# Polysketch attention into a SwiGLU block: the exact 12-bit parts a batch earlier

## Chip, cores and metric

The kernel runs on one core of one Trainium2 chip. The metric is the device time of one execution in microseconds (us). Before the change it is 293.77 us, the median of 3 runs (292.49 to 293.79); the execution that was profiled took 292.29 us, of which the span from first to last instruction is 290.6 us.

## What is computed

Four batches, four heads, 1088 tokens, head size 32. A sketch of rank 8 gives 64 features per token and head; attention with these is linear, and its result x (4352 tokens of 128) goes through a gated feed-forward block of 1536 hidden columns. All inputs and outputs are fp32.

```python
def phi(x):
    a = np.einsum('rd,bhsd->bhsr', S1, x)
    b = np.einsum('rd,bhsd->bhsr', S2, x)
    return np.einsum('bhsi,bhsj->bhsij', a, b).reshape(*x.shape[:-1], r * r)
kv = np.einsum('bhsf,bhsd->bhfd', k_p, v)
z = np.sum(k_p, axis=2)
num = np.einsum('bhsf,bhfd->bhsd', q_p, kv)
den = np.einsum('bhsf,bhf->bhs', q_p, z)[..., None] + 1e-06
# x = (num / den), heads side by side, 4352 x 128
g = x @ w_gate
silu = g * (1.0 / (1.0 + np.exp(-g)))
val = x @ w_val
return silu * val @ w_out
```

## The kernel before

**Blocks, units, downs.** Each batch of tokens is cut into three blocks of 384, 384 and 320 tokens, so that there are twelve; the 1536 hidden columns are twelve chunks of 128. A *unit* is one chunk of one block: a gate product and a value product on TensorE, SiLU on ScalarE, and their product into a slot of `hbuf`. A *down* (L936) multiplies a finished hidden chunk with its 128 rows of `w_out` and adds into the PSUM bank `acc`; after twelve downs of a block, `store` (L967) transposes the bank on VectorE and sends it out. The list `todo` holds hidden chunks that wait for their down, and a lag says how many may wait.

**Three kinds of unit.** `unit` (L903, matmuls at L911) makes both products in true fp32; SiLU is L917, and VectorE multiplies it with the value straight out of PSUM (L928). `cut_unit` (L868) makes a product from parts that hold 12 bits each[...]: a product of differences `xd` by `wd` (L877), then `x1` by `w1` and `x0` by `wb` (L883, L884), which ScalarE (L889) and VectorE (L892) put together into `sum`. With `both=False` only the value is made so and the gate stays fp32 (L879); with `both=True` both are. In either case GpSimd multiplies SiLU and value into `hbuf` (L901)[...]. The parts of weights come from `cut_weights` (L835), four steps for each of four quarter weights: `w1` on ScalarE, `low` on GpSimd, `wb` on ScalarE, `wd` on GpSimd. Those of a block's tokens come from `cut_tokens` (L850): `x1` on ScalarE, `x0` on a given engine (L859), and, after a yield, `xd` on VectorE (L863).

**Banks and buffers.** [...] At first units take g0, g1, g2 (and `acc`) in turn, and `a` and `b`, two banks each, belong to attention. Once `oldest[0]` is set, `bank` (L110) gives the bank that was handed out longest ago among those not held. A `cut_unit` takes three banks, or four with both products. `sg`, SiLU's output, has three buffers.

**Order.** The schedule is by hand[...]. The first batch's units are mixed with its attention and with the reading of the weights; from its 18th unit of the list at L1137 on, each unit has one down. The 23 downs that are left run three at a time in the loop at L1160. Then comes the loop of units at L1177, y = 0 to 107, over the blocks 3, 4, 5, 6, 7, 8, 9, 11, 10.

Attention of the batches 1 to 3 is the generator `attentions` (L563), of which `parts_of` (L1087) runs a piece at a time between units: `turns` (transposes of keys and queries), `features` (key features, L355), `feature_sums` (L521, sums of key features over token groups, four adds on GpSimd), and `query_step` (L706: query products with the sums at L719, reduces at L726, small operations at L735 to L741, feature products at L355 and transposes at L750). When it yields "pe", it has come to work for TensorE: `group` (L1093) then runs `numerators` (L760, matmuls L770, copies into `xT` at L787), `values` (key-value products L366, and L678, which reads the sums `zs`), sketches of the next batch (L332, L320) and `spread_out` (L683). The token columns of a batch after its first 384 exist only after that group. "first" is the mark after the numerators of the second batch's first 384 tokens; before, the loop of downs stops at it.

The three groups stand ahead of y = 12, 36 and 60. Units y < 38 are plain; y 38 to 47 have the value in parts, y 48 to 106 both, and y 107 is plain. The lag is 2 up to y 37 and 5 after. Value weights are cut from y 2, gate weights from y 14. `oldest[0]` is set at y 36.

```python
PLAIN, VALUE = 3 * NCH + 2, 4 * NCH
...
    if y in (NCH, 3 * NCH, 5 * NCH):
        group()
...
    if y < PLAIN or y == END - 1:
        unit(i, j)
    else:
        cut_unit(i, j, both=y >= VALUE)
    lag = LAG if y < PLAIN else min(5, END - y + 1)
```

Of the kernel before, what the change touches and what calls it, by code (L numbers as in the profile page):

```python
# [7 lines left out]
FP32 = mybir.dt.float32  # L8
# [4 lines left out]
AF = mybir.ActivationFunctionType  # L13
ALU = mybir.AluOpType
# [5 lines left out]
def kernel(  # L20
# [28 lines left out]
    nc = tc.nc  # L49
    P = nc.NUM_PARTITIONS  # L50
# [6 lines left out]
    NC = (NX + 3) // 4  # L57
    F = R * R
    NCH = Dff // P
# [7 lines left out]
    steps = [(sum(plan[:s]), n) for s, n in enumerate(plan)]  # L67
# [13 lines left out]
    fpool = ctx.enter_context(tc.tile_pool(name="ffn", bufs=2))  # L81
# [10 lines left out]
    oldest = [False]  # L92
# [41 lines left out]
    wg = const.tile([P, NCH, P], FP32, name="wg")  # L134
# [151 lines left out]
    def run(*gens):  # L286
        for g in gens:
            for _ in g:
                pass
# [231 lines left out]
    def feature_sums(phk):  # L521

        rows = phk[:].rearrange("p c h i j -> p c (h i j)")
        s = apool.tile([P, 4, H * F], FP32, tag="zs", name="zs")
        add = lambda o, a, b: nc.gpsimd.tensor_tensor(out=o, in0=a, in1=b, op=ALU.add)  # L525
        add(s[:], rows[:, 0:4, :], rows[:, 4:8, :])
        add(s[:, 0:2, :], s[:, 0:2, :], s[:, 2:4, :])
        add(s[:, 0, :], s[:, 0, :], s[:, 1, :])
        add(s[:, 0, :], s[:, 0, :], rows[:, 8, :])
        return s[:, 0, :]  # L530

    def turns(b):

        for c in kpieces:
            turn_k(*c)
            if c[1] == NC and b + 1 < B:
                load_k(b + 1)
            yield
        for x0, x1 in ((0, 4 * kpieces[0][1]), (4 * kpieces[0][1], 4 * NC)):
            nc.vector.transpose(out=qT[:, x0:x1, :], in_=qld[:, x0:x1, :])  # L540
            if x1 == 4 * NC and b + 1 < B:
                load_q(b + 1)
            yield
# [19 lines left out]
    def attentions():  # L563
# [25 lines left out]
        for n, (i, c0, c1) in enumerate(((0, 0, 3), (0, 3, 5), (1, 5, 7), (1, 7, 9))):  # L589
# [11 lines left out]
                release("a")  # L601
            if n % 3 != 1:
                yield
        zs = feature_sums(phk)
        for i, _ in enumerate(turns(2)):
            if i % 2:
                yield
# [18 lines left out]
        phk = hbuf[:, NH - 6 :, :].rearrange("p s (n h i j) -> p (s n) h i j", h=1, i=R, j=R)  # L626
        phk = phk.rearrange("p (c h) o i j -> p c (h o) i j", h=H)
        yield from features(phk, fac2, ())
        zs = feature_sums(phk)
        yield from turns(3)  # L630
        yield "pe"
        numerators(1, spread, 3, NC)
        hold("a", "b")
# [2 lines left out]
        kp, qp = wide("a"), wide("b")  # L636
        fac3, copies = sketches([(c0, c1, kp[:, i], qp[:, i]) for i, (c0, c1) in enumerate(kpieces)])
        spread = spread_out(2, kv)
        run_copies(copies, 2)
        yield  # L640
        run_copies(copies, 2)
        release("a", "b")
        yield
        yield from features(phk, fac3, ())
        zs = feature_sums(phk)
        yield from query_step(2, fac2, spread)(0, NC)
        yield "pe"
        numerators(2, spread, 0, NC)
        kv = bank()
# [145 lines left out]

    LAG = 2
    hidden = {}
    acc = {}  # L800
    todo = []
# [14 lines left out]
    def whole(ap):  # L816
        return ap.bitcast(FP32)
# [14 lines left out]
                for k in range(2):  # L832
                    yield [x[:, k] for x in t]

    def cut_weights(w, at, steps):  # L835

        def put(at, f, **args):
            steps.setdefault(at, []).append(lambda: f(**args))  # L838

        for c, (w1, wb, wd) in enumerate(homes(w)):  # L840
            src = w[:, 3 * c : 3 * c + 3, :]
            low = fpool.tile([P, 3, P], FP32, tag="sgl", name="low", bufs=6)[:]
            w_parts[id(w), c] = (w1, wb, wd)
            sub = dict(op=ALU.subtract)
            put(at + c, nc.scalar.activation, out=w1, in_=src, func=AF.Copy, scale=CUT)
            put(at + 4 + c, nc.gpsimd.tensor_tensor, out=low, in0=src, in1=whole(w1), **sub)
            put(at + 12 + c, nc.scalar.activation, out=wb, in_=low, func=AF.Copy, scale=BETA)
            put(at + 16 + c, nc.gpsimd.tensor_tensor, out=wd, in0=whole(w1), in1=whole(wb), **sub)

    def cut_tokens(i, engine=nc.gpsimd):  # L850

        t0, n = blocks[i]
        x = xT[:, t0 : t0 + n]
        x1, x0, xd = x_parts[i] = [
            apool.tile([P, BW], F32R, tag=tag, name=name, bufs=2)
            for tag, name in (("qb", "x1"), ("dT", "x0"), ("rd", "xd"))
        ]
        nc.scalar.activation(x1[:, 0:n], x, AF.Copy, scale=CUT)
        engine.tensor_tensor(  # L859
            out=x0[:, 0:n], in0=x, in1=whole(x1[:, 0:n]), op=ALU.subtract  # L860
        )
# [221 lines left out]

    att = attentions()
    ahead = [None]

    def parts_of(n):  # L1087

        for _ in range(n):
            if ahead[0] not in ("pe", "end"):  # L1090
                ahead[0] = next(att, "end")

    def group():  # L1093
        while ahead[0] != "pe":
# [45 lines left out]
    for z, (i, j) in enumerate(seq):  # L1140
        if z == 17:
            free_banks.pop()
            turn[0] %= 4
        unit(i, j)
        for p in parts.get(z, ()):
            part(*p)
        if z in (24, 25, 26):
            catch_up()
        if z == 6:
            load_k(1)  # L1150
            load_v(1, [nc.sync] * 4)
# [23 lines left out]
    coming_x = iter(())  # L1175
    cutting = {}
    for y in range(END):  # L1177
        i, j = line[y // NCH], y % NCH
        if y in (NCH, 3 * NCH, 5 * NCH):
            group()  # L1180
        if y == 3 * NCH:
            oldest[0] = True
            hold("acc")
            run(cut_tokens(i, nc.vector))
# [9 lines left out]
        for w, at in ((wv, 2), (wg, 14)):  # L1194
            if y == at:
                cut_weights(w, at, cutting)
        for step in cutting.pop(y, ()):
            step()
        if j == 4 and 3 * NCH < y < END - NCH:
            coming_x = cut_tokens(line[y // NCH + 1])  # L1200
        if j in (4, 6):
            next(coming_x, None)
    ps = wide("a")[:, 0, 0:D]
    for j in range(NCH):
        if todo and j % 4 == 0:
# [40 lines left out]
```

## Time and profile before

Busy time of the engines in stretches of the span (us; the clock granted to TensorE is 1.00 in each but the last, 0.98):

| stretch (us) | what runs | TensorE | VectorE | ScalarE | GpSimd |
|---|---|---|---|---|---|
| 77.3 to 92.6 | the 23 downs left of the first batch | 15.30 | 6.24 | 0.89 | 0.00 |
| 92.6 to 114.6 | y 0 to 11, plain | 22.00 | 20.43 | 7.53 | 7.41 |
| 114.6 to 119.8 | first group | 4.98 | 0.74 | 1.55 | 2.31 |
| 119.8 to 143.3 | y 12 to 23, plain | 23.50 | 17.71 | 9.76 | 14.52 |
| 143.3 to 162.85 | y 24 to 35, plain, 320 tokens | 19.55 | 12.85 | 6.89 | 4.39 |
| 162.85 to 165.6 | second group | 2.75 | 0.75 | 0.70 | 0.00 |
| 165.6 to 185 | y 36 to 47 | 19.40 | 15.98 | 11.41 | 11.37 |
| 185 to 206.7 | y 48 to 59, both in parts | 21.25 | 17.94 | 16.41 | 15.47 |

Each row sets the length of a stretch beside what the engines did in it. TensorE is busy nearly all the time, so a stretch is about as long as TensorE's work in it; the other engines' columns say how much room they have. A mean over a stretch hides the order within it, so single waits have to be looked up in the timeline of an engine. Busy times of TensorE are modelled at the ends of matmuls; the distance from one start to the next is the firmer number.

### The profile page before, as it was taken

Reading aid. Unit: us, or ns where it says so; the run is one execution under the profiler, and the core shown is the slowest. Engines: PE = TensorE matmul, PEld = TensorE weight load, DVE = VectorE, ACT = ScalarE, POOL = GpSimd, SP = SyncE. Lnnn points to the kernel's source line nnn. Section 1 sums busy time; section 2 is a strip of 40 time slices with the busy share of each in tenths; the row PEclk is TensorE's granted clock in tenths of the full one; section 3 lists DMA queues with packets and bytes.
Section 4 is the critical chain, followed back from the end, with each engine's and each line's share of the span. In section 5 each row is a group of like instructions: output and inputs, shape, how many; then the busy total and the mean of one; then the engine's idle time right before and its main releaser. Section 6 shows DMA issues by size and latency. Waiting matters only on the chain.

```text
span 290.6 us, 6170 instructions
## 1 busy us (share of the span) xinstructions
PE 284.5 (98%) x2307; PEld 204.6 (70%) x2307; DVE 200.7 (69%) x400; ACT 154.5 (53%) x369; POOL 130.1 (45%) x144
## 2 busy tenths in 40 slices
PE   8899999999999999999999999999999999999995
PEld 7545566667666555755667677778788988888985
DVE  3997988875542997188893369997567675676651
ACT  3567565431301432353242365578688888888860
POOL 3215322138000308039741039676466676576650
PEclk9999999999999999999999999999999999999999
DMA  7564292315411100140010020001001010020101
GB/s 199 153 211 111 61 314 72 103 55 162 115 20 26 17 0 2 34 104 0 0 28 3 2 50 0 2 0 27 2 1 28 2 23 0 0 32 0 24 2 27
DMA packets 26142, 14.63 MB, mean 50 GB/s; under 512 B 18688, under 2 KB 24192, under 8 KB 26112
## 3 DMA queue, kind: packets, MB, share of 16 engines
q1 hardware_dynamic: 25456, 14.13, 19.1%
q8 instruction: 18, 0.29, 0.4%
q10 hardware_dynamic: 656, 0.10, 0.2%
q14 instruction: 12, 0.10, 0.1%
HBM read 11.41 MB, written 2.23 MB: 47 GB/s over the span
## 4 chain that ended last, share of the span: by engine, by line
PE 91%; DVE 3%; DMA 1%; issue 1%; ACT 1%; POOL 0%; SPq 0%; DVEq 0%
PE PS L911 32%; PE PS L942 28%; PE PS L877 7%; PE PS L883 7%; PE PS L884 7%; PE PS L879 2%; PE PS L770 2%; PE PS L332 2%; PE PS L366 2%; DMA kld<-in_k_dram 1%; PE PS L320 1%; DVE sum L892 1%; PE PS L957 1%; PE PS L475 1%; PE PS L423 1%
## 5 line engine op out<-in xcount | busy, mean ns | idle before, releaser
L942 PE MATMUL PS<-hbuf,wo 128*128 128x384 f32 (+2 forms) x288 | 104.7, 460 | 0.4 <-DVE o L971 0.4
L901 POOL TENSOR_TENSOR hbuf<-sg,sum 128x384 f32<-128x384 f32 (+1 forms) x69 | 69.8, 1015 | 53.6 <-ACT sg L896 31.4
L892 DVE SCALAR_TENSOR_TENSOR sum<-PS,sum 128x384 f32<-128x384 f32 (+1 forms) x128 | 62.7, 527 | 29.4 <-ACT sum L889 27.1
L917 ACT ACTIVATE sg<-PS 128x384 f32<-128x384 f32 (+1 forms) x75 | 35.4, 473 | 68.5 <-PE PS L911 66.1
L942 PEld LDWEIGHTS PS<-hbuf,wo 128*128 128x128 f32 x288 | 52.5, 189 | 17.6 <-issue 0.7
L911 PE MATMUL PS<-xT,wg 128*128 128x384 f32 (+1 forms) x150 | 59.1, 476 | 0.0
L911 PE MATMUL PS<-xT,wv 128*128 128x384 f32 (+1 forms) x150 | 58.3, 470 | 0.2 <-DVE wv L270 0.2
L889 ACT ACTIVATE sum<-PS 128x384 f32<-128x384 f32 (+1 forms) x128 | 53.3, 465 | 5.6 <-PE PS L877 5.2
L928 DVE TENSOR_TENSOR hbuf<-sg,PS 128x384 f32<-128x384 f32 (+1 forms) x69 | 36.1, 524 | 28.6 <-PE PS L911 26.8
L911 PEld LDWEIGHTS PS<-xT,wv 128*128 128x128 f32 x150 | 28.3, 190 | 17.9 <-DVE hbuf L928 0.9
L911 PEld LDWEIGHTS PS<-xT,wg 128*128 128x128 f32 x150 | 27.6, 190 | 18.2 <-issue 1.2
L896 ACT ACTIVATE sg<-sum 128x384 f32<-128x384 f32 (+1 forms) x59 | 29.7, 503 | 17.2 <-DVE sum L892 16.5
L877 PE MATMUL PS<-xd,gphq 128*128 128x384 f32 (+1 forms) x59 | 34.6, 587 | 0.0
L883 PE MATMUL PS<-x,w 128*128 128x384 f32 (+1 forms) x69 | 25.4, 368 | 0.0
L877 PE MATMUL PS<-xd,wd 128*128 128x384 f32 (+1 forms) x69 | 24.6, 357 | 0.0
L884 PE MATMUL PS<-x,wb 128*128 128x384 f32 (+1 forms) x69 | 22.6, 328 | 0.0
L883 PE MATMUL PS<-x,graw 128*128 128x384 f32 (+1 forms) x59 | 19.2, 325 | 0.0
L884 PE MATMUL PS<-x,graw 128*128 128x384 f32 (+1 forms) x59 | 19.1, 324 | 0.0
L877 PEld LDWEIGHTS PS<-xd,wd 128*128 128x128 f32 x69 | 13.1, 189 | 6.8
L838 POOL TENSOR_TENSOR low<-wv,w 128x384 f32<-128x384 f32 x4 | 4.7, 1176 | 25.4 <-ACT w L838 25.4
L877 PEld LDWEIGHTS PS<-xd,gphq 128*128 128x128 f32 x59 | 11.1, 189 | 6.4 <-issue 0.4
L525 POOL TENSOR_TENSOR zs<-hbuf 128x1024 f32<-128x1024 f32 x2 | 4.7, 2364 | 21.5 <-PE PS L911 11.6
(129 smaller groups left out, 340.7 us busy)
## 6 DMA issues: line engine op xcount, KB each, us to landing
kld<-in_k_dram SPq DMA_DIRECT2D x4, 544.0 KB, 4.2
vld<-in_v_dram SPq DMA_DIRECT2D x12, 144.0 KB, 4.8
qld<-in_q_dram SPq DMA_DIRECT2D x3, 544.0 KB, 3.8
raw<-in_moe_w_out_dram SPq DMA_DIRECT2D x4, 384.0 KB, 3.7
out_dram<-o SPq DMA_DIRECT2D x28, 48.0 KB, 1.9
raw<-in_moe_w_gate_dram SPq DMA_DIRECT2D x3, 384.0 KB, 3.2
raw<-in_moe_w_val_dram SPq DMA_DIRECT2D x3, 384.0 KB, 3.3
out_dram<-o SPq DMA_DIRECT2D x16, 40.0 KB, 1.7
```

What stands on the lines that cost most here:

```text
L332: nc.tensor.matmul(ps[32 * a : 32 * a + 64, 64 * (c - c0) : 64 * (c - c0) + 64], kT[:, c, a : a + 2, :].rearrange("p a t -> p (a t)"), s12 ...
L877: nc.tensor.matmul(d, wd, xd, start=True, stop=True)
L883: nc.tensor.matmul(p, w1, x1, start=True, stop=False)
L884: nc.tensor.matmul(p, wb, x0, start=False, stop=True)
L889: nc.scalar.activation(s, d, AF.Copy, scale=-1.0 / BETA)
L892: nc.vector.scalar_tensor_tensor(out=s, in0=p, scalar=1.0 + 1.0 / BETA, in1=s, op0=ALU.mult, op1=ALU.add)
L896: nc.scalar.activation(sg, sums[0] if both else g, AF.Silu)
L901: nc.gpsimd.tensor_tensor(out=hj[:, 0:n], in0=sg, in1=sums[-1], op=ALU.mult)
L911: nc.tensor.matmul(o[:, 0:n], w[:, j, :], xT[:, t0 : t0 + n], start=True, stop=True)
L917: nc.scalar.activation(sg[:, 0:n], g[:, 0:n], AF.Silu)
L928: nc.vector.tensor_tensor(out=hj[:, 0:n], in0=sg[:, 0:n], in1=u[:, 0:n], op=ALU.mult)
L942: nc.tensor.matmul(acc[i][:, 0:n], wo[:, j, :], hidden[i, j][:, 0:n], start=(j == 0), stop=(j == NCH - 1),)
```

## The change

It gives the value products of the second batch (y 0 to 35) exact 12-bit parts too, and the gates from y 31 on instead of y 48, so that fewer products are made in true fp32. What these need is made earlier: the value weights are cut from the 25th unit of the first batch's list to the second pass of the downs (two of the four `low` on VectorE), and block 3's tokens during the downs. So that VectorE has less to do beside the units of the second batch, the loop of downs runs two pieces of attention a pass, and goes on past "first".

The groups now stand ahead of y = 10, 30 and 60. `oldest[0]` is set, and `acc` held, from y 0; the lag is 5 from the start. The feature sums of the third and the fourth batch are four steps that go out one by one beside `turns` or `query_step`; for all three batches the first add of 1024 elements is now two of 512. Gate weights are cut from y 8, into four slots of `hbuf` (units keep 17 of 27). Token parts of block 4 are made at y 10 and 11 with the first subtraction on VectorE, those of block 5 at y 16 and 18, of block 6 at y 30 and 32, and so on. From y 36 on attention goes on in odd y alone. In the first group the four copies of sketches follow each other with no unit between.

```diff
-        add(s[:], rows[:, 0:4, :], rows[:, 4:8, :])
-        add(s[:, 0:2, :], s[:, 0:2, :], s[:, 2:4, :])
...
+        return s[:, 0, :], [
+            lambda: add(s[:, 0:2, :], rows[:, 0:2, :], rows[:, 4:6, :]),
+            lambda: add(s[:, 2:4, :], rows[:, 2:4, :], rows[:, 6:8, :]),
+            lambda: add(s[:, 0:2, :], s[:, 0:2, :], s[:, 2:4, :]),
+            last,
+        ]
+
+    def beside(gen, steps):
+
+        for x in gen:
+            if steps:
+                steps.pop(0)()
+            yield x
...
-        zs = feature_sums(phk)
-        yield from turns(3)
+        zs, sums = feature_sums(phk)
+        yield from beside(turns(3), sums)
...
-        run_copies(copies, 2)
-        yield
-        run_copies(copies, 2)
+        run_copies(copies, 4)
...
-        zs = feature_sums(phk)
-        yield from query_step(2, fac2, spread)(0, NC)
+        zs, sums = feature_sums(phk)
+        yield from beside(query_step(2, fac2, spread)(0, NC), sums)
...
+        if z == 24:
+            lows = [fpool.tile([P, 3, P], FP32, tag="sgl", name="low", bufs=6)[:] for c in range(4)]
+            engines = [nc.vector] * 2 + [nc.gpsimd] * 2
+            first, low, second, third = cut_weights(wv, list(zip(engines, lows)))
+        if z in (25, 26):
+            take(first, 2)
+        if z == 27:
+            take(low, 4)
     todo.sort()
+    x_steps = None
     while todo:
         for _ in range(min(3, len(todo))):
             down()
-        if ahead[0] != "first":
-            parts_of(1)
-    while ahead[0] != "first":
+        take(second, 2)
+        take(third, 2)
+        if begun[0]:
+            x_steps = x_steps or cut_tokens(HEAD, nc.vector)
+            next(x_steps, None)
+        parts_of(2 if len(todo) > 6 else 1)
+    while not begun[0]:
         parts_of(1)
-
-    slots[:] = range(NH - 6)
+    run(x_steps or cut_tokens(HEAD, nc.vector))
+
+    slots[:] = range(NH - 10)
...
-    PLAIN, VALUE = 3 * NCH + 2, 4 * NCH
...
+    GROUPS, GATES = (10, 30, 60), 31
+
+    token_steps = {}
+    for m, i in enumerate(line[1:], 1):
+        y = max(NCH * (m - 1) + 4, *(g for g in GROUPS if g < NCH * m))
+        gen = cut_tokens(i, nc.vector if m == 1 else nc.gpsimd)
+        for at in (y, y + (1 if m == 1 else 2)):
+            token_steps.setdefault(at, []).append(gen)
+    oldest[0] = True
+    hold("acc")
+    lows = [hbuf[:, NH - 10 + c, :].rearrange("p (c f) -> p c f", f=P) for c in range(4)]
...
-        if y < PLAIN or y == END - 1:
+        if y == END - 1:
             unit(i, j)
         else:
-            cut_unit(i, j, both=y >= VALUE)
-        lag = LAG if y < PLAIN else min(5, END - y + 1)
+            cut_unit(i, j, both=y >= GATES)
         for _ in range(2):
-            if len(todo) > lag:
+            if len(todo) > min(5, END - y + 1):
                 down()
-        parts_of(2 if y in (0, 4, 6, 7, 8) else 1)
...
+        parts_of(y < 36 or y % 2)
+        if y == 8:
+            gate_rows = cut_weights(wg, [(nc.gpsimd, low) for low in lows])
+        for n, row in enumerate(gate_rows):
+            if y >= 8 + (0, 4, 12, 16)[n]:
+                take(row, 1)
+        for gen in token_steps.get(y, ()):
+            next(gen, None)
```

More of the change, by code (lines that the diff above doesn't have):

```diff
@@ L525, in feature_sums, with last @@
         add = lambda o, a, b: nc.gpsimd.tensor_tensor(out=o, in0=a, in1=b, op=ALU.add)
-        add(s[:], rows[:, 0:4, :], rows[:, 4:8, :])
-        add(s[:, 0:2, :], s[:, 0:2, :], s[:, 2:4, :])
-        add(s[:, 0, :], s[:, 0, :], s[:, 1, :])
-        add(s[:, 0, :], s[:, 0, :], rows[:, 8, :])
-        return s[:, 0, :]
+        def last():
+            add(s[:, 0, :], s[:, 0, :], s[:, 1, :])
+            add(s[:, 0, :], s[:, 0, :], rows[:, 8, :])
+        return s[:, 0, :], [
[9 more added lines that the diff above has]
+            yield x
     def turns(b):
@@ L603, in attentions @@
                 yield
-        zs = feature_sums(phk)
+        zs, sums = feature_sums(phk)
+        for f in sums:
+            f()
         for i, _ in enumerate(turns(2)):
@@ L644, in attentions @@
         yield from features(phk, fac3, ())
-        zs = feature_sums(phk)
-        yield from query_step(2, fac2, spread)(0, NC)
+        zs, sums = feature_sums(phk)
+        yield from beside(query_step(2, fac2, spread)(0, NC), sums)
         yield "pe"
@@ L794, in query_runs @@
         return zip(cuts, cuts[1:])
-    LAG = 2
+    HEAD = len(steps)
     hidden = {}
@@ L833, in homes, with cut_weights, take @@
                     yield [x[:, k] for x in t]
-    def cut_weights(w, at, steps):
-        def put(at, f, **args):
-            steps.setdefault(at, []).append(lambda: f(**args))
+    def cut_weights(w, lows):
+        rows = [], [], [], []
+        sub = dict(op=ALU.subtract)
         for c, (w1, wb, wd) in enumerate(homes(w)):
             src = w[:, 3 * c : 3 * c + 3, :]
-            low = fpool.tile([P, 3, P], FP32, tag="sgl", name="low", bufs=6)[:]
+            engine, low = lows[c]
             w_parts[id(w), c] = (w1, wb, wd)
[L844 to L848, printed above, removed]
+            for row, f, args in zip(
+                rows,
+                (nc.scalar.activation, engine.tensor_tensor, nc.scalar.activation, nc.gpsimd.tensor_tensor),
+                (
+                    dict(out=w1, in_=src, func=AF.Copy, scale=CUT),
+                    dict(out=low, in0=src, in1=whole(w1), **sub),
+                    dict(out=wb, in_=low, func=AF.Copy, scale=BETA),
+                    dict(out=wd, in0=whole(w1), in1=whole(wb), **sub),
+                ),
+            ):
+                row.append((f, args))
+        return rows
+    def take(steps, n):
+        for _ in range(n):
+            if steps:
+                f, args = steps.pop(0)
+                f(**args)
     def cut_tokens(i, engine=nc.gpsimd):
@@ L1085 @@
     ahead = [None]
+    begun = [False]
     def parts_of(n):
@@ L1091, in parts_of @@
                 ahead[0] = next(att, "end")
+                begun[0] |= ahead[0] == "first"
     def group():
@@ L1173 @@
     END = len(line) * NCH
-    PLAIN, VALUE = 3 * NCH + 2, 4 * NCH
-    coming_x = iter(())
-    cutting = {}
+    GROUPS, GATES = (10, 30, 60), 31
[8 more added lines that the diff above has]
+    lows = [hbuf[:, NH - 10 + c, :].rearrange("p (c f) -> p c f", f=P) for c in range(4)]
@@ L1177 @@
+    gate_rows = []
     for y in range(END):
         i, j = line[y // NCH], y % NCH
-        if y in (NCH, 3 * NCH, 5 * NCH):
+        if y in GROUPS:
             group()
[L1181 to L1184, printed above, removed]
-        if y < PLAIN or y == END - 1:
+        if y == END - 1:
             unit(i, j)
         else:
-            cut_unit(i, j, both=y >= VALUE)
-        lag = LAG if y < PLAIN else min(5, END - y + 1)
+            cut_unit(i, j, both=y >= GATES)
@@ L1190 @@
         for _ in range(2):
-            if len(todo) > lag:
+            if len(todo) > min(5, END - y + 1):
                 down()
-        parts_of(2 if y in (0, 4, 6, 7, 8) else 1)
[L1194 to L1202, printed above, removed]
+        parts_of(y < 36 or y % 2)
```

## The prediction, made before the change was run

> A unit is one hidden chunk of one token block; y counts units from the start of the second batch (y 0 to 107).
>
> **What bounds the kernel now.** I read the page first: TensorE is busy 284.5 of 290.6 us (98%), at full granted clock, VectorE 69%, ScalarE 53%, GpSimd 45%. The chain that ended last names TensorE for 91%. So the time is TensorE's own work plus its holes, and the price of a unit can be read off the chain in order of time (start, us, what):
>
> ```profile
> 129.72 1.29 PE PS L911 x4
> 131.01 0.65 PE PS L942 x2
> 131.65 1.29 PE PS L911 x4
> ...
> 182.22 0.64 PE PS L879 x2
> 183.21 0.65 PE PS L942 x2
> 184.03 0.65 PE PS L879 x2
> ...
> 199.27 0.65 PE PS L942 x2
> 200.96 0.65 PE PS L942 x2
> ```
>
> With 384 tokens a plain unit and one down take 1.93 us (129.72 to 131.65), a unit with its value product in parts 1.81, one with both in parts 1.69. With 320 tokens the chain has 1.61 for plain (158.01 to 159.62) and 1.42 for both; value alone at 320 never occurs, and lies between them: 1.51.
>
> Next I read the other engines' timelines, as a faster TensorE leans on their order. VectorE during the first batch's downs, and the shape of its later pieces (start, us, work, idle before):
>
> ```profile
> 80.82 0.26 DVE L741 TENSOR_TENSOR qab<-qab,den 128x96 f32<-128x96 f32 x1
> 85.06 0.58 DVE L971 STREAM_TRANSPOSE o<-PS 128x384 f32<-128x384 f32 x1 [3.98 <-PE PS L942]
> ...
> 107.60 1.89 DVE L355 TENSOR_TENSOR hbuf<-kabs 128x512 f32<-128x512 f32 x3
> ```
>
> It waits in order: the store of block 1 keeps it idle 4 us though query features stand behind it. And GpSimd:
>
> ```profile
> 112.10 2.08 POOL L525 TENSOR_TENSOR zs<-zs 128x512 f32<-128x512 f32 x2
> ...
> 171.47 1.00 POOL L901 TENSOR_TENSOR hbuf<-sg,sum 128x384 f32<-128x384 f32 x1 [17.42 <-ACT sum L889]
> 175.15 1.73 POOL L859 TENSOR_TENSOR x<-xT,x 128x384 fp32r<-128x384 f32 x1
> 188.06 1.51 POOL L901 TENSOR_TENSOR hbuf<-sg,sum 128x384 f32<-128x384 f32 x1 [0.65 <-ACT sg L896]
> ```
>
> Before the parts begin it has nothing to do in a unit (17 us idle); from then on each unit costs it one 1.0 us product, which can stretch to 1.5 or more.
>
> [...] 0.645 us for an fp32 product of 384 tokens, 0.16 to 0.17 from one part product to the next. [...] the products of 1.51 us stand beside line 355's VectorE products, others take 1.00. I take 0.5 us for each such meeting.
>
> **The change, what TensorE saves.** y 0 to 23, plain to value parts at 384: 24 x 0.12 = 2.9. y 24 to 30, at 320: 7 x 0.10 = 0.7. y 31 to 35, plain to both: 5 x 0.19 = 0.95. y 36, 37: 2 x 0.24 = 0.5. y 38 to 47, value to both: 10 x 0.12 = 1.2. Sum 6.3. Two holes of before also go: 0.5 ahead of y 12 (119.35 to 119.84) and 0.6 near 195, where a store is late behind query features on VectorE (its downs are 2.31 apart, not 1.69). Later units get no cheaper. In all 7.4.
>
> **What it costs, in order.**
>
> 1. The second batch's sums, during the first batch's units, start with two adds of 512 (GpSimd has 2.08 for 512 + 256 and 0.73 for 256, so 1.35 each) in place of one of 1024 (2.36). Its sums were just in time: 0.3 longer, and TensorE waits 0.2.
>
> 2. During the 23 downs the query features come two pieces at a time. Those ahead of the first numerators use the 4 us hole (VectorE done at 83.0, TensorE there at 83.7): free. The rest stand behind block 1's store (85.9 on TensorE). From there to the sum of y 5, by spacings in the trace: store 0.5; token parts 0.5 + 0.5; two query products and reduces 3.7; the small operations 1.9; four feature products and transposes 0.9 each, 3.6; second store 0.5; key features 0.9 + 3 x 0.63 = 2.8; six sums at 0.47, 2.8: 16.8, so till 102.7. TensorE needs 12 downs at 0.54 and six units at 1.17 (no down yet; the chain has 170.81 to 171.97), 13.5, and 0.8 more to that sum: 100.2. VectorE is 2.5 late. With 7 banks and 3 a unit, a sum's bank is wanted again two units later; y 3 to 5 wait a little: 0.4 in all (0 to 1.2), 2.1 late left.
>
> 3. Sums of the third batch, on GpSimd at y 5 to 8, each behind a hidden product. From the sum of y 5: 4 x 0.96 + 3 x 1.35 + 1.5 = 9.4. TensorE from the end of y 5 to the small product that reads them (group at y 10): 4 x 1.81 + down 0.65 + banks 0.2 + numerators 1.16 + key products 1.03 = 10.3; with 0.8 for the sum it would fit by 0.1. VectorE's lateness is therefore passed on: wait 2.0 (0 to 3).
>
> 4. Both groups' numerators now share banks with running units. The third group, which already did, took 1.69 where the second took 1.48: 0.2 each, 0.4.
>
> 5. Token parts of block 4. Its values exist only after y 10's group, and y 12 begins with the product that reads them. The last subtraction stands on VectorE behind y 11's sum and two key features: 0.3 + 0.47 + 2 x 0.63 + 0.6 = 2.6 after y 11's end, of which one down (0.65) is cover: wait 2.0 (1.6 to 2.3).
>
> 6. y 12 to 17 on GpSimd: hidden products, four gate cuts from y 12, the fourth batch's sums in four steps from y 13, block 5's subtraction at y 16. Up to that: 5 x 0.96 + 4 x 0.96 + 5.55 + 0.96 = 15.2, from 1.0 after y 12's end. VectorE's next step for block 5, queued at y 18, waits for it, and the sums of y 19, 20 behind it with the small query operations (2.3): 16.2 + 0.55 + 0.47 + 2.3 + 0.47 = 20.0 after y 12. TensorE wants the bank of y 20's sum at y 23's start, 10 x 1.81 + 0.65 = 18.75. Wait 1.3 if nothing contends, 2.8 with three meetings; I take 1.6.
>
> 7. Query features of the last batch beside units with both parts: the small operations (2.3) may hold 4 of 7 banks: 0.2 (0 to 1).
>
> Costed at nothing: ScalarE's extra copy, 0.49 a unit of 1.81, leaves it 0.98 busy; weight cuts at y 25 to 27 of the first batch find VectorE idle (70.8 to 73.9) and GpSimd free after 72; the third group and all after it are as before.
>
> Sum: 0.2 + 0.4 + 2.0 + 0.4 + 2.0 + 1.6 + 0.2 = 6.8. Net 7.4 - 6.8 = 0.6 saved: 293.77 - 0.6 = 293.2.
>
> **Rivals.** *Gain kept* (0.38): VectorE is not late, so step 3 falls to 0, step 6 to 1.3 or less, step 2 to 0: costs 4.1, 3.3 saved, 290.5; with step 6 at 0 as well, 289.2. For it: TensorE's holes give the others time, and in y 38 to 47 it already ran value parts with query features at 1.81 with no hole. Against: there GpSimd had no sums or cuts beside them. *GpSimd is the new bound* (0.20): each piece of step 6 meets VectorE more often (11 pieces from 171.5 to 187.4 took 13.9 us, not 11), step 6 gives 4, step 3 gives 3, steps 2 and 7 give 1 each: costs 11.6, 4.2 slower, 298.0; half of the excess gives 295.6. [...] *They cancel* (0.42): as worked out, 293.2.
>
> **How the numbers follow.** The likeliest is that they cancel, 293.2; below 292.3 is the first rival, above 295.2 the second. Low 289.6 and high 295.8 leave out the far ends of both.
>
> **What would show it.** TensorE's timeline after: 1.81 a unit from y 5, about 1.51 at 320, 1.69 from y 36; a hole of 2 us ahead of the product that reads the sums in the first group, released by GpSimd line 525's adds; one of 2 ahead of y 12, released by VectorE's token subtraction; one or two at y 22 and 23, released by VectorE sums standing behind that subtraction and GpSimd. If the first is missing, step 2 has overrated VectorE; if the third is larger, contention was. It would be wrong altogether if the part products ran slower than in y 38 to 59.

## The result, and the profile after

The changed kernel takes 305.15 us (median; 303.3 to 306.61), the kernel before, on the same chip, 293.2 (292.49 to 293.79). The ratio is 1.0405, interval 1.0341 to 1.047: it is 12 us slower. Its four executions took 303.3, 305.01, 305.29 and 306.61 us at mean granted clocks of 0.989, 0.983, 0.982 and 0.978; the last of them is the one that was profiled. The prediction was 293.2, with a range up to 295.8. It was wrong, and on the side of the rival that was given the smallest chance.

The page of the changed kernel, busy time of the engines, and the granted clock in 40 slices:

```profile
PE 285.1 (94%) x2362; PEld 214.4 (70%) x2362; DVE 213.5 (70%) x423; ACT 177.5 (58%) x427; POOL 170.2 (56%) x185
...
PEclk9799999999999997879999999999999999999999
```

TensorE has less arithmetic to do and is busy 0.6 us longer than before, in a span 14 us longer. The last row gives one reason: the granted clock, 9 throughout before, has 7s and an 8 in it. (The 7 at the left belongs to this execution: its keys landed 0.7 us later than before, TensorE waited 1.46 us for them, and from 7.6 to 15 us it ran at a mean clock of 0.77. That start cost it some 1.7 us that the other kernels below did not pay. So comparisons are made from y 0 on.)

TensorE's timeline after, from 80 us on: the rows that began after a wait of 0.9 us or more, the first products of y 0, y 8 and y 9, and the numerators of the third group (start, us, work, then idle time and who ended it):

```profile
86.74 0.96 PE L783 MATMUL PS<-phT,spread 32*32 32x96 f32 x64 [1.00 <-DVE phT L763]
...
95.25 0.58 PE L903 MATMUL PS<-xd,wd 128*128 128x384 f32 x1
...
107.37 0.63 PE L903 MATMUL PS<-xd,wd 128*128 128x384 f32 x1
...
109.18 0.63 PE L903 MATMUL PS<-xd,wd 128*128 128x384 f32 x1
...
116.25 0.32 PE L691 MATMUL PS<-zs,ones 128*32 128x64 f32 x8 [2.48 <-POOL zs L525]
116.50 1.95 PE L332 MATMUL PS<-s,kT 128*64 128x64 f32 x36
118.38 2.08 PE L320 MATMUL PS<-s,qT 128*32 128x64 f32 x72
...
127.73 0.66 PE L903 MATMUL PS<-xd,wd 128*128 128x384 f32 x1 [3.46 <-DVE xd L889]
128.19 1.48 PE L905 MATMUL PS<-xT,wg 128*128 128x384 f32 x2
...
151.25 0.44 PE L903 MATMUL PS<-xd,wd 128*128 128x384 f32 x1 [2.17 <-DVE sum L918]
...
154.25 0.44 PE L903 MATMUL PS<-xd,wd 128*128 128x384 f32 x1 [0.92 <-DVE sum L918]
...
209.16 0.88 PE L968 MATMUL PS<-hbuf,wo 128*128 128x384 f32 x2 [0.92 <-DVE o L997]
...
220.13 1.57 PE L783 MATMUL PS<-phT,spread 32*32 32x288 f32 x64
```

The same sketches before, and the two rows from which the stretch below is counted:

```profile
92.41 0.81 PE L911 MATMUL PS<-xT,wg 128*128 128x384 f32 x2
...
116.94 1.27 PE L332 MATMUL PS<-s,kT 128*64 128x64 f32 x36
118.14 1.21 PE L320 MATMUL PS<-s,qT 128*32 128x64 f32 x70
...
206.62 1.76 PE L770 MATMUL PS<-phT,spread 32*32 32x288 f32 x64
```

A unit does cost 1.81 (107.37 to 109.18), as worked out. The three waits of the first group, of y 12 and of y 22 and 23 stand where the prediction put them, released by the lines that it named. They are larger: 2.48, 3.46 and 2.17 + 0.92 in place of 2.0, 2.0 and 1.6. And there is a thing that it did not have at all: behind the first two, TensorE itself is slow. The sketches of L332 and L320 take 1.95 and 2.08 where the same rows took 1.27 and 1.21 before, and the gate products of L905 in y 12 and y 13 take 1.48 each where 0.81 is the rule. The busy times of the changed kernel by stretches show the clock (last columns: granted clock, share of the DMA, GB/s):

```profile
116.20:118.00 1.80, 1.75 (x40) 1.66 (x42) 0.25 (x1) 0.57 (x2) 0.96 (x1) 0.68 0.00 0
118.00:120.40 2.40, 2.40 (x83) 2.19 (x79) 0.00 (x0) 0.86 (x3) 0.00 (x0) 0.53 0.17 44
120.40:124.20 3.80, 3.80 (x18) 2.46 (x14) 2.25 (x3) 3.34 (x8) 1.55 (x1) 1.00 0.34 89
...
129.00:131.00 2.00, 2.00 (x7) 1.40 (x5) 0.58 (x2) 0.49 (x1) 0.00 (x0) 0.50 0.00 0
```

About half speed after each of the two long waits, for some 4 and some 6 us, and full speed between. The chain of waits shows what stands behind them, in order of time:

```profile
114.72 0.68 POOL zs L525
...
116.25 0.32 PE PS L691 x8
...
125.12 2.00 DVE hbuf L355 x2
127.12 0.48 DVE xd L889
127.73 0.66 PE PS L903
...
142.25 1.72 POOL hbuf L927
...
148.57 0.87 POOL x L885
```

Before, this chain was TensorE for 91%; now it is 78%, VectorE 8% and GpSimd 7%. From 122 to 127.6 it runs through VectorE's key features and token parts, from 134.6 to 149.4 through GpSimd almost without a break.

One measure is free of the start: the time from the first product of y 0 to the numerators of the third group (60 units and two groups). It is 114.21 us before (92.41 to 206.62) and 124.88 after (95.25 to 220.13). The rest of the kernel, from there to the end, is 83.98 and 84.47.

### The profile page after: what moved, and what is told of

Same layout as the page of the kernel before. It is cut to its first block, busy times and chain, and to the rows that moved or that the text cites. A ratio compares the mean times of both kernels' runs of the same rounds, so it can differ in the third digit from the quotient of the medians.

```text
span 304.6 us, 6491 instructions
## 1 busy us (share of the span) xinstructions
PE 285.1 (94%) x2362; PEld 214.4 (70%) x2362; DVE 213.5 (70%) x423; ACT 177.5 (58%) x427; POOL 170.2 (56%) x185
## 4 chain that ended last, share of the span: by engine, by line
PE 78%; DVE 8%; POOL 7%; issue 3%; DMA 2%; ACT 0%; SPq 0%; DVEq 0%; POOLq 0%
PE PS L968 23%; PE PS L937 15%; PE PS L903 10%; PE PS L909 9%; PE PS L910 9%; PE PS L905 4%; POOL hbuf L927 3%; POOL zs L525 3%; PE PS L332 2%; DVE sum L918 2%; DMA kld<-in_k_dram 2%; PE PS L320 1%; DVE hbuf L355 1%; PE PS L783 1%; PE PS L366 1%
## 5 line engine op out<-in xcount | busy, mean ns | idle before, releaser
L927 POOL TENSOR_TENSOR hbuf<-sg,sum 128x384 f32<-128x384 f32 (+1 forms) x107 | 113.9, 1067 | 73.8 <-ACT sg L922 40.7
L918 DVE SCALAR_TENSOR_TENSOR sum<-PS,sum 128x384 f32<-128x384 f32 (+1 forms) x183 | 90.1, 527 | 45.0 <-ACT sum L915 30.5
L915 ACT ACTIVATE sum<-PS 128x384 f32<-128x384 f32 (+1 forms) x183 | 77.1, 464 | 22.3 <-PE PS L903 21.5
L903 PE MATMUL PS<-xd,wd 128*128 128x384 f32 (+1 forms) x107 | 42.6, 398 | 6.8 <-DVE xd L889 3.5
L909 PE MATMUL PS<-x,w 128*128 128x384 f32 (+1 forms) x107 | 44.6, 417 | 0.0
L937 PE MATMUL PS<-xT,wv 128*128 128x384 f32 (+1 forms) x74 | 28.8, 472 | 0.2 <-DVE wv L270 0.2
L905 PE MATMUL PS<-xT,wg 128*128 128x384 f32 (+1 forms) x62 | 25.6, 497 | 0.0
L909 PEld LDWEIGHTS PS<-x,w 128*128 128x128 f32 x107 | 20.5, 191 | 4.6 <-issue 0.6
L954 DVE TENSOR_TENSOR hbuf<-sg,PS 128x384 f32<-128x384 f32 (+1 forms) x31 | 16.2, 524 | 10.7 <-PE PS L937 9.9
L910 PEld LDWEIGHTS PS<-x,wb 128*128 128x128 f32 x107 | 20.5, 192 | 4.0 <-issue 0.6
L937 PEld LDWEIGHTS PS<-xT,wv 128*128 128x128 f32 x74 | 13.9, 190 | 9.1 <-DVE hbuf L954 0.9
```

Of the source, the lines that this page charges most:

```text
L903: nc.tensor.matmul(d, wd, xd, start=True, stop=True)
L905: nc.tensor.matmul(g, wg[:, j, :], xT[:, t0 : t0 + n], start=True, stop=True)
L909: nc.tensor.matmul(p, w1, x1, start=True, stop=False)
L910: nc.tensor.matmul(p, wb, x0, start=False, stop=True)
L915: nc.scalar.activation(s, d, AF.Copy, scale=-1.0 / BETA)
L918: nc.vector.scalar_tensor_tensor(out=s, in0=p, scalar=1.0 + 1.0 / BETA, in1=s, op0=ALU.mult, op1=ALU.add)
```

## Experiments

The last column is the start of y 0, in us from the start of the span.

| kernel | median us | y 0 to third numerators | y 0 starts at |
|---|---|---|---|
| before | 293.2 | 114.21 | 92.41 |
| after | 305.15 | 124.88 | 95.25 (start 1.7 late) |
| e1_filled | 301.63 | 121.16 | 93.60 |
| e2_tokens4 | 301.38 | 121.47 | 93.46 |
| e3_sums | 298.94 | 119.47 | 93.37 |
| e4_tokens5 | 302.57 | 122.61 | 93.34 |
| e5_plain | 294.04 | 114.62 | 93.46 |
| e6_features | 301.55 | 119.74 | 94.79 |
| v1_moved | 295.0 | 116.12 | 92.71 |
| v2_moved | 292.34 | 110.32 | 94.83 |
| v3_later | 290.3 | 110.95 | 93.20 |

The theory drawn from this profile had two parts. *Clock*: behind the holes of 2.48 and 3.46 us TensorE ran at about half speed (granted clock 0.68 to 0.53, and 0.50), which costs about 4.3 us beyond the holes (1.95 + 2.08 for 1.27 + 1.21 in the sketches, and 6.39 for 3.62 in y 12 and 13). *Queues*: the holes themselves come from VectorE and GpSimd, which got the copies, sums and cuts of the parts, and whose operations take longer side by side (VectorE's two key features 2.07 at 125.04, 0.63 each before; GpSimd's hidden product 1.72 at 142.25, where others take 1.00). The rival to the clock: the slow products are slow because they read what others write at that moment, and would be so without a hole. The rival to the queues: the new order (groups at y 10 and 30, features among the downs) makes the holes whatever the units are.

### e1_filled: products without use in the two longest holes

```diff
+        if fill[0]:
+            idle_bank(fill[0])      # 12 products of 512 into a free bank
         for h in range(H):
             nc.tensor.matmul(
                 kv[32 * h : 32 * h + 32, F : 2 * F], ones[:], zs[...],
...
+        if y == 12:
+            idle_bank(16)
```

> The changed kernel with 12 dummy products (32x512, bf16) ahead of the small products that read the third batch's sums and 16 ahead of y 12, so that TensorE has work in its two longest holes (2.5 and 3.5 us) while the waits themselves stay. Theory A (a hole of this length halves the granted clock for what follows): the clock stays at 1.00 through both places, the sketches after the first take about 2.4 us again and not 3.9, y 12 and 13 take 3.6 and not 6.4, so about 4 us less than the changed kernel, near 301. Theory B (what follows the holes is slow for another cause, such as banks or operands shared with the other engines): the two stretches stay slow and the time stays within 1 us of the changed kernel, 305.

301.63 us (301.38 to 301.89), ratio 1.0292 [1.0261, 1.0323]. TensorE's timeline of it at the two places:

```profile
111.95 2.77 PE L225 MATMUL PS<-const-bfloat16-1.0 128*32 128x512 bf16 x12
114.61 0.32 PE L699 MATMUL PS<-zs,ones 128*32 128x64 f32 x8
114.86 1.27 PE L332 MATMUL PS<-s,kT 128*64 128x64 f32 x36
116.05 1.21 PE L320 MATMUL PS<-s,qT 128*32 128x64 f32 x72
...
121.02 3.65 PE L225 MATMUL PS<-const-bfloat16-1.0 128*32 128x512 bf16 x16
124.61 0.45 PE L911 MATMUL PS<-xd,wd 128*128 128x384 f32 x1
```

The sums and the tokens come as late as before; only the waiting is done with products. The sketches are back at 1.27 and 1.21, y 12 and 13 at 1.63 and 1.81, and the clock is 9 in every slice. The gain is 3.5 us in the medians and 3.72 from y 0 to the third numerators. So the clock is shown to be a cost of its own, beside the holes, of a little under the 4.3 that was added up; 0.7 of the 4.3 is given back in y 14 to 23, to which TensorE now comes sooner (22.43 us in place of 21.75). The rival to it falls: the same products read the same tiles at the same distance from VectorE's writes, at full speed.

### e2_tokens4: block 4's token parts ahead of the attention of y 10

```diff
+        if m == 1:
+            first_gen = gen
+            continue
...
+        if y == 10:
+            run(first_gen)          # both steps, before parts_of
         parts_of(y < 36 or y % 2)
```

> The changed kernel with both steps of block 4's token parts issued at y 10, ahead of that unit's piece of attention; nothing else is moved. Theory A: the hole ahead of y 12 (3.5 us) goes and with it the half clock of y 12 and 13 (2.7 us): about 6 us less, near 299. Theory B: 3.5 us less, near 301.5. A third, that the wait only moves on to y 22, where GpSimd is late anyway: less than 2 us gained, above 303.

301.38 (301.13 to 301.96), ratio 1.0286 [1.0248, 1.0325]. The hole ahead of y 12 falls from 3.46 to 0.21, and its half clock goes with it. But not all of it is kept. TensorE's timeline:

```profile
122.68 0.41 PE L903 MATMUL PS<-xd,wd 128*128 128x384 f32 x1 [0.21 <-DVE xd L889]
...
138.78 0.44 PE L909 MATMUL PS<-x,w 128*128 128x384 f32 x1 [0.54 <-ACT sg L922]
...
141.93 0.44 PE L909 MATMUL PS<-x,w 128*128 128x384 f32 x1 [1.06 <-ACT sg L922]
...
145.48 0.44 PE L903 MATMUL PS<-xd,wd 128*128 128x384 f32 x1 [2.29 <-DVE sum L918]
```

TensorE comes to y 20 earlier, GpSimd doesn't: two waits on SiLU's three buffers, which GpSimd empties, are new ahead of the 2.29, and this time the 2.29 is followed by half clock (the granted clock is 0.50 from 147 to 149 us). The gain is 3.8 us in the median where the hole and its slow products alone were 6.0. y 14 to 23 take 24.57 in place of 21.75. Step 5 of the prediction had the right wait; what is given back later belongs to GpSimd.

### e3_sums: the third batch's sums cut to one add

```diff
-        yield from beside(turns(3), sums)
+        short = lambda: nc.gpsimd.tensor_tensor(out=zs, in0=few[:, 0, :], in1=few[:, 8, :], op=ALU.add)
+        yield from beside(turns(3), [lambda: None] * 3 + [short])
```

> The changed kernel with the third batch's key-feature sums cut down to one add of two of the nine groups (the other groups are left out of that batch's denominators). GpSimd then has 0.7 us of sums at y 8 and not 5.3 from y 5 on. Theory A: the wait ahead of the products that read the sums (2.5 us) goes and with it the half clock of the sketches (1.5 us): about 4 us less, near 301. Theory B: 2.5 us less, near 302.5. If VectorE's lateness and not GpSimd's queue were what holds that place: no change, 305.

298.94 (298.66 to 299.06), ratio 1.0199 [1.0168, 1.0229]. Four adds of five are left out here, so that the third batch's normalizers are those of two token groups alone; the run measures what waits for the adds. The hole of 2.48 is gone and the sketches take 1.27 and 1.21. The hole of 3.46 ahead of y 12 stays, but its half clock is shorter: y 12 takes 3.03 (121.63 to 124.66) and y 13 2.03, together 5.06 and not 6.39. In all 6.2 us in the median, 5.41 from y 0 on: 2.5 of hole, 1.5 of sketches, 1.3 of y 12 and 13. The last part was not expected, and it isn't shown to come from the edit: e4, which changes nothing ahead of the hole, has the same 5.06 for y 12 and 13. The same hole of 3.46 costs 2.8 us of slow products in one execution and 1.4 in others.

### e4_tokens5: block 5's first step at y 12

```diff
-        for at in (y, y + (1 if m == 1 else 2)):
+        for at in ((12, 18) if m == 2 else (y, y + (1 if m == 1 else 2))):
...
+        if y == 12:
+            for gen in token_steps.pop(y):
+                next(gen, None)
```

> The changed kernel with the first step of block 5's token parts (ScalarE copy and GpSimd subtraction) issued at y 12, ahead of the gate cuts and sums, and no longer at y 16 behind them; the second step stays at y 18. If VectorE's wait for that subtraction makes the holes at y 22 and 23 (2.6 and 1.2 us): both go, about 3.5 us less, near 301.5. If GpSimd's backlog holds TensorE there by itself, through the three buffers of SiLU outputs: less than 1.5 us gained, above 303.5.

302.57 (302.12 to 303.9), ratio 1.0332 [1.0293, 1.037]. VectorE no longer waits for GpSimd's subtraction. TensorE still waits, now inside y 21 and 22, and ScalarE's timeline says for what. The first products of y 12, 13 and 14 stand ahead:

```profile
125.87 0.50 PE L903 MATMUL PS<-xd,wd 128*128 128x384 f32 x1 [3.46 <-DVE xd L889]
...
128.79 0.96 PE L903 MATMUL PS<-xd,wd 128*128 128x384 f32 x1
...
130.93 0.63 PE L903 MATMUL PS<-xd,wd 128*128 128x384 f32 x1
...
145.81 0.44 PE L909 MATMUL PS<-x,w 128*128 128x384 f32 x1 [0.91 <-ACT sg L922]
...
149.08 0.44 PE L909 MATMUL PS<-x,w 128*128 128x384 f32 x1 [1.18 <-ACT sg L922]
```

```profile
141.66 0.49 ACT L922 ACTIVATE sg<-PS 128x384 f32<-128x384 f32 x1 [2.32 <-POOL hbuf L927]
...
148.53 0.49 ACT L922 ACTIVATE sg<-PS 128x384 f32<-128x384 f32 x1 [2.39 <-POOL hbuf L927]
```

SiLU has no buffer until GpSimd has made its product. So the token subtraction was one of two ways in which GpSimd's backlog of these units reaches TensorE; with it gone the backlog comes through `sg`. The gain is 2.6 in the median (the intervals of the two ratios overlap) and 2.27 from y 0 on, but little of it belongs to the edit. y 14 to 23 take 20.76 in place of 21.75, so 1.0 of the 3.6 lost there comes back. The other 1.3 is the shorter half clock in y 12 and 13 (125.87 to 130.93, 5.06 in place of 6.39), behind a hole that the edit leaves as it was. That is nearer to the second of the two expectations: GpSimd's backlog holds TensorE there by itself.

### e5_plain: the changed order, but y 0 to 30 plain

```diff
-        if y == END - 1:
+        if y == END - 1 or y < GATES:
             unit(i, j)
```

> The changed kernel with y 0 to 30 as plain fp32 units again (the arithmetic of that part undone); groups, sums, cuts and token steps stay where the change put them. If the holes come from what the parts add on GpSimd and VectorE in a row with the rest: a plain unit has no hidden product on GpSimd, block 4 needs no token parts at y 12 and no sum waits for block 5's, so the four holes (2.5, 3.5, 2.6, 1.2 us) and the 4.3 us of half clock go, while 31 units cost 3.6 us more: about 295. If the holes come from the moved groups and from the order alone: they stay, and the time rises by the 3.6 us, to about 308.

294.04 (293.77 to 294.28), ratio 1.0051 [1.0036, 1.0065]. All cuts, sums and token parts are still made, and everything stands where the change put it. Only the units of y 0 to 30 are two fp32 products again, so that VectorE has one product a unit and GpSimd none. The holes at y 12, 22 and 23 go, the one in the first group falls to 1.24 (and is no longer released by the sums), the clock is 1.00. From y 0 to the third numerators it is 114.62, against 114.21 before. The parts in 31 units, which save TensorE about 3.6 us, add 10.3. So the rival to the queues falls for the holes at y 12, 22 and 23. The order isn't free, though: the units from y 31 on keep their saving here (0.95 + 0.5 + 1.2 by the prediction's prices), so order and early cuts cost some 3.1 us between y 0 and the third numerators (0.4 and the saving of 2.65), and 1.0 ahead of y 0. The wait of 1.24 and two waits for stores, 0.94 at 175.39 us and 0.95 at 197.10, are the visible part; before had one wait for a store there, of 0.45.

### e6_features: key features of the third batch on GpSimd, in the downs

```diff
         yield "first"
-        yield from step(3, NC)
...
-        yield from features(phk, fac2, ())
+        for c0, c1 in ((0, 3), (3, 5), (5, 7), (7, 9)):
+            ...
+            key_features(phk, (kab[:, 0, x, :], kab[:, 1, x, :]), c0, c1, nc.gpsimd)
+        yield from step(3, NC)
```

> The changed kernel with the third batch's four key-feature products on GpSimd, issued during the first batch's downs where GpSimd is idle, and no longer on VectorE at y 2 to 4; sums start where they did in the generator's order, which is now three units earlier. If VectorE's lateness after the downs is what reaches TensorE through the sums: VectorE has 2.8 us less ahead of y 5, the wait at the first group (2.5 us) and the half clock behind it (1.5 us) go, as does the 0.3 at y 7: about 4 to 5 us less, near 300.5. If GpSimd's own queue from y 5 to 8 is too long whatever VectorE does: the wait stays, and the time with it, 304 to 305.

Here the features are written into six hidden chunks of the first batch before their downs have read them, so those rows of the output come from other data. Number, size and order of the instructions are those that are meant.

301.55 (301.0 to 301.79), ratio 1.0305 [1.029, 1.032]. The wait for the sums in the first group is gone: with 2.8 us taken off VectorE the hidden products that GpSimd waited for come in time. So step 3's reason, VectorE's lateness passed on to GpSimd, is right. But the numerators before y 0 now start 1.3 us later. TensorE's timeline, and VectorE's ahead of it:

```profile
86.29 0.96 PE L786 MATMUL PS<-phT,spread 32*32 32x96 f32 x64 [2.26 <-DVE phT L766]
```

```profile
82.94 2.21 DVE L355 TENSOR_TENSOR phq<-qab 128x768 f32<-128x768 f32 x1
```

The feature product of 768 that stands alone in 0.95 takes 2.21 beside GpSimd's key features. From y 0 on 5.1 us are gained, and 1.3 are given back ahead of it. Of the 5.1, 1.5 is again a shorter half clock in y 12 and 13 (4.87), which the edit doesn't touch.

### v1_moved: all of these places moved at once

e6's key features, e2's token parts, block 5's parts at y 12 and 14, `wd` of the value weights behind "first", gate weights cut in later steps (rows from y 8, 18, 22, 26), and attention in every unit from y 36 but two. The same six chunks are overwritten as in e6.

```diff
-            if y >= 8 + (0, 4, 12, 16)[n]:
+            if y >= 8 + (0, 10, 14, 18)[n]:
...
-        parts_of(y < 36 or y % 2)
+        parts_of(y not in (39, 40))
```

> All places mended at once, the arithmetic of the change kept: key features as in e6_features; the last step of the value weights' cuts behind the first numerators; block 4's token parts at y 10 ahead of attention; block 5's at y 12 and 14; gate weights' low, second copy and last step from y 18, 22 and 26; attention in every unit but y 39 and 40. If the saving on TensorE is as worked out (6.3 us for the units, 1.7 for holes of the kernel before) and only waits and the half clock ate it: no hole over 0.5 us up to y 60, clock 1.00, about 286 to 288. If the units with parts themselves are dearer in the second batch than where the kernel before has them, or a wait only moves on: 293 or more.

295.0 (294.83 to 295.09), ratio 1.0082 [1.0065, 1.0099]. The clock is 1.00 and from y 0 on no hole is longer than 0.95 us, but it missed what was expected: small waits of 0.5 to 0.95, most of them at y 24 to 29 (SiLU's buffers again, as the cuts now stand there) and in y 36 to 59 (sums and stores behind query features). From the second to the third numerators it takes 56.0 us, and the changed kernel 54.04. That speaks for one part of the change, attention in odd units alone; as the cuts moved too, it isn't shown by itself.

### v2_moved: moved further

From v1: gate weights cut at y 3 to 10 with `low` on VectorE, block 4's token parts right after its numerators, at most one piece of attention a pass in the last downs, attention mostly in odd units from y 36, with a few gaps, and the features' buffer put on chunks that have had their downs. The lines taken out are those of the changed kernel.

```diff
-            gate_rows = cut_weights(wg, [(nc.gpsimd, low) for low in lows])
+            gate_rows = cut_weights(wg, [(nc.vector, low) for low in lows])
         for n, row in enumerate(gate_rows):
-            if y >= 8 + (0, 4, 12, 16)[n]:
-                take(row, 1)
+            if y >= (3, 5, 8, 9)[n]:
+                take(row, 1 if n < 2 else 2)
...
         numerators(1, spread, 3, NC)
+        run(cut_tokens(HEAD + 1, nc.vector))
```

> The arithmetic of the change with the order mended further, from the trace of v1_moved: the third batch's key features on GpSimd in the six slots of hbuf that are free by then; fewer pieces of attention in the last two passes of the downs; block 4's token parts inside the first group, right behind the numerators; gate cuts at y 3 to 10 with low on VectorE, so that GpSimd has no cuts from y 12 on; no attention in y 15, and from y 36 in odd y except 39 and 51, with 56. If the units' saving is as worked out and the queues of GpSimd and VectorE are what ate it: y 12 to 29 run at 1.81 and 1.62 with less than 1 us of holes, y 36 to 59 at 1.69 with less than 0.7, about 287. If GpSimd is too full from y 12 to 29 even so (18 hidden products, sums, block 5's subtraction, with contention): 2 to 3 us of holes stay there, about 290. If it only moves on: 293 or more.

292.34 (290.71 to 294.07), ratio 0.9987 [0.9965, 1.0008]: as long as before. Its twenty executions fall into two groups: seven of 290.7 to 291.1 us at a mean granted clock of 1.00, and thirteen of 291.9 to 294.1 at 0.994. The trace is of the first group, so where the others lost their clock isn't shown. From y 0 to the third numerators it takes 110.32, 3.9 less than before, and y 10 to 29 run without a hole at 1.81 and 1.62. But y 0 starts 2.4 later. Its numerators wait 2.35 us, as in e6: GpSimd had nothing left to wait for and ran the key features from 80.8, under VectorE's small operations.

```profile
80.78 5.34 POOL L355 TENSOR_TENSOR hbuf<-kabs 128x768 f32<-128x768 f32 x4
```

```profile
81.25 1.08 DVE L756 TENSOR_SCALAR den<-den 128x12 f32<-128x12 f32 x1
...
83.48 1.71 DVE L355 TENSOR_TENSOR phq<-qab 128x768 f32<-128x768 f32 x1
```

### v3_later: v2 with the key features held back by the queue

```diff
         yield "first"
+        x_steps.append(cut_tokens(HEAD, nc.gpsimd))
+        next(x_steps[0])
         phk = hbuf[:, 0:6, :]...
```

Block 3's first subtraction, which reads the numerators' result, goes to GpSimd ahead of the features. They stand behind it in GpSimd's queue: it waits 4.39 us for its input, and they start at 87.80, when it ends. The `wd` of the value weights also go out a pass earlier than in v2.

> v2_moved with one place changed: block 3's first token subtraction (x0) is issued on GpSimd right after the first numerators and ahead of the third batch's key features, so that these can't begin before the numerators have reached xT; the wd of the value weights are issued a pass earlier. Contention theory (the 2.35 us hole at 86.3 in v2_moved is VectorE's small operations and its L355 of 1.71 us stretched by the GpSimd key features that run beside them): the hole falls to 1.0 or less, as in the changed kernel, the numerators start at about 85, VectorE is late by at most 1 us in y 0 to 5, and the time is 290.7 to 291.5, a little under both kernels. Rival (GpSimd's queue is the limit there: key features that end 8 us later push the hidden products and sums back): the hole goes but 1.5 to 2.5 us come back as waits up to the first group, and the time stays at 292 to 293.

290.3 (290.1 to 290.89), ratio 0.9917 [0.9901, 0.9932]: faster than both kernels, by 2.4 us (2.0 to 2.9) than the one before. GpSimd's and TensorE's timelines:

```profile
86.84 1.00 POOL L891 TENSOR_TENSOR x<-xT,x 128x384 fp32r<-128x384 f32 x1 [4.39 <-ACT x L890]
87.80 6.34 POOL L355 TENSOR_TENSOR hbuf<-kabs 128x768 f32<-128x768 f32 x4
```

```profile
84.70 0.96 PE L789 MATMUL PS<-phT,spread 32*32 32x96 f32 x64 [1.00 <-DVE phT L769]
...
110.24 1.19 PE L789 MATMUL PS<-phT,spread 32*32 32x160 f32 x60 [1.19 <-DVE sum L924]
```

The numerators wait 1.00 in place of 2.35, and y 0 starts 1.6 earlier. VectorE's feature product, now ahead of GpSimd's, takes 0.96 where v2 had 1.71. VectorE pays for the features a little later: the last subtraction of block 3's token parts takes 0.89 at 89.56 us (in v2, with GpSimd idle, 0.55 at 91.61). The first group waits 1.19 where v2 had 0.32. The hole went as the contention theory had it, and 0.9 of it came back at the first group as the rival had it, though not the 1.5 to 2.5 that it named. From v2 the span is 1.0 us shorter, the median 2.0. All six executions of v3 are at clocks of 0.998 to 1.00, and against v2's seven of that kind it gains only some 0.5; the rest is that v3 has no executions at 0.994. A wait of 2.35 that brings half clock in some executions and not in others would explain it, as holes of 2.29 brought it in e2 and e6 and not in e1 and e3; for v2 it isn't shown. Waits of 1.00, 1.19, 0.51 and 0.75 are still in it.

## Why the prediction was wrong

More than one step failed. First, a term that the sum put at nothing: TensorE's clock after a hole. The runs showed 3.5 to 4.3 us of slow products behind two holes. Second, steps 5 and 6 priced VectorE and GpSimd too low when both are busy; they came out 1.5 and 2.0 us longer.

Its sum for y 0 to the third numerators was 114.21 - 7.4 + 6.6 = 113.4 (step 1 lies ahead of y 0), measured 124.88: 11.5 over. Point by point, measured against predicted:

- **What TensorE saves** holds as far as unit prices go: 1.81 at 384, 1.62 with a down of 384 beside 320 tokens (0.10 less than plain, as worked out), 1.42 for both at 320 (170.22 to 171.64). It would have been "wrong altogether" if part products ran slower there; at full clock they do not. v2 and v3 collect 3.9 and 3.3 of it. That the store's hole of 0.6 would go was wrong: it came back as two, in y 36 to 59.
- **Step 1** (0.2): nothing; from the first gate product to the 23 downs both kernels take 61.98 us (15.14 to 77.12, and 17.14 to 79.12).
- **"Free"**, the query features in the 4 us hole: 1.0. The hole was there, but two small operations did not keep their size beside GpSimd's `wd`: 0.91 and 0.74 for 0.26 each.
- **Step 2** (0.4): y 0 to 9 take 16.1 where five units alone at 1.17 and five with a down at 1.81 make 14.9, so 1.2; only 0.26 of it is a wait that the timeline names.
- **Step 3** (2.0): 2.48, with the reason that was given (e6).
- **Step 4** (0.4): about 0.2. From the last down to the numerators the first group takes 0.74 (before 0.73), the second 0.85 (before 0.63).
- **Step 5** (2.0): 3.46. The formula had every term, 0.3 + 0.47 + 2 x 0.63 + 0.6, with the sizes of VectorE alone. VectorE's timeline shows what became of them:

```profile
122.42 0.95 DVE L355 TENSOR_TENSOR hbuf<-kabs 128x768 f32<-128x768 f32 x1
123.29 1.36 DVE L885 TENSOR_TENSOR x<-xT,x 128x384 fp32r<-128x384 f32 x1
124.58 0.55 DVE L918 SCALAR_TENSOR_TENSOR sum<-PS,sum 128x384 f32<-128x384 f32 x1
125.04 2.07 DVE L355 TENSOR_TENSOR hbuf<-kabs 128x512 f32<-128x512 f32 x2
```

  The `x0`, 0.52 when GpSimd stands idle (v2), took 1.36 and made y 11's sum late; the two key features took 2.07 and not 1.26. GpSimd made hidden products at the same time.
- **Step 6** (1.6, 1.3 to 2.8): 3.6 in y 14 to 23. From y 12's product to block 5's subtraction it had 15.2 us on GpSimd; they were 18.3 (131.12 to 149.43). Five hidden products took 7.3 for 4.8, and 1.3 is idle time while TensorE made y 13 at half clock. e4 adds what the step did not see: SiLU's three buffers bind TensorE to GpSimd even where no subtraction does (waits of 0.91 and 1.18).
- **Step 7** and the store: 1.9 (0.76 + 0.92 + 0.23) for 0.2.
- **The term that was missing**: half clock after the holes of steps 3 and 5, 1.55 + 2.77 = 4.3 in the execution that was profiled. By e1, 3.5 to 3.7. It is the largest single miss.

The excesses (0.8, 0.5, -0.2, 1.5, 2.0, 1.7, 4.3) are 10.6 of the 11.5; 0.9 is not placed. With 1.0 ahead of y 0 and 0.5 after the third numerators, the three stretches are 12.2 longer than before; the medians differ by 12.0.

So the balance "saves 7.4, costs 6.8" treated holes as idle time at their own length, and durations from the trace of before, where GpSimd stood idle for 17 us at a time, as if they held beside a busy GpSimd. The rival that made GpSimd the new bound had the right cause. It had step 6 right in size (4 for 3.6) and step 3 (3 for 2.5), yet gave 298.0, since it too left out the clock and left step 5 at 2.0.

The missing term stands in the trace after: a hole of 3.46 us was followed by a granted clock of 0.50, and one of 2.48 by 0.68 and then 0.53. The prediction's own holes, two of 2.0 with ranges to 3 and 2.3, were priced at their length alone; the runs show that the two holes that came cost more than that. The trace of before could not show it, having no hole over 0.5 us behind its first microsecond. For the other half, the prediction priced 0.5 us for a meeting, on GpSimd's side alone. In the traces of the runs VectorE paid too: 0.65 (0.91 for 0.26), 0.8 (1.36 for 0.52) and 1.26 (2.21 for 0.95) in one instruction. That the two engines stretch each other is read off their timelines in steps 5 and 6; one place was tested by moving the work, in v3, and there the size came back (0.96 for v2's 1.71).

## What to carry to other kernels

Before work is moved off the bounding engine onto two others, take the durations of the receiving engines from a stretch where both are busy, and count each instruction twice: for its own time, and for what it adds to its neighbour. Here a subtraction of 0.52 us became 1.36 on VectorE, and five hidden products worked out at 4.8 became 7.3 on GpSimd. The length of a predicted hole in TensorE need not be its whole price: here holes of 2.48 and 3.46 us cost another 1.5 and 1.3 to 2.8 in slow products, and filling them with products of no use won 3.5 us. When an operation only needs to be late, put it in its engine's queue behind one that has to wait; that took a wait of 2.35 us down to 1.00, and the median from that of the kernel before to 2.4 us under it.

## What the runs showed of the hardware

- The length of a hole alone does not tell whether half clock follows. It came behind holes of 2.48 (after: 0.68, then 0.53; e4: 0.85, then 0.50) and 2.49 (e2: 0.79, then 0.50), and behind those of 3.46 (0.50 in after and e6, 0.52 in e3, 0.54 in e4, in the first 1.3 to 2.1 us). After holes of 2.29 it came in e2 and e6 (0.50 from 147 to 149 us) and not in e1 (1.00 from 145.8 to 151 us) and e3 (gate products of 0.81 at 144.24 and 147.23, as at full clock). After 2.17 (after), 2.26 (e6) and 2.35 (v2, the execution profiled) it did not come: 1.00 from 151.2 to 158, from 86.2 to 93 and from 86 to 94.8 us. At the start of the changed kernel it came after 1.46 us alone (0.50 from 8 to 11 us); v2 waited 1.24 us there, and its mean clock over the span is 1.00. What decides it was not shown.
- How long it lasts varies too: y 12 and 13 after the same hole of 3.46 took 6.39 us in the changed kernel, 5.06 in e3 and e4 and 4.87 in e6; e4's edit touches nothing ahead of the hole. In the four executions of the changed kernel, mean clocks of 0.989 to 0.978 go with 303.3 to 306.61 us: 0.011 of some 305 us is 3.4, and the times differ by 3.3.
- Some VectorE operations with two tensor inputs took longer beside GpSimd's: 0.91 for 96 elements in after (81.78 us, 0.26 before), 2.21 for 768 in e6 (82.94 us, 0.95 alone). Not all did: a product of 768 took 0.96 in v3 (87.69 us). An operation on 12 elements with one tensor input was slow too, 1.08 where before had 0.17 (v2, L756); why was not settled.
